# Three small redistributions by way of DRAM instead of TensorE products, in a gated mix of two attention blocks

## The chip, the cores and the metric

The kernel runs on one core of one Trainium2 chip. The metric is the device time of one execution in microseconds (us); lower is better. Before and after are compared by the median of several executions. A profile of one execution gives the times of single instructions. TensorE (PE) does the matrix products and its weight loads (PEld), VectorE (DVE) and ScalarE (ACT) drain its results from PSUM, GpSimd (POOL) works on SBUF, and SyncE (SP) issues nearly all DMA transfers, in one queue.

## The reference

Two full attention blocks run on the same `x` (2048 rows of 640) with their own weights, 32 heads of 20 features each; a sigmoid gate mixes the two results.

```python
def _A_ref(x, wqkv, wo):                      # _B_ref is the same
    qkv = (x @ wqkv).reshape(B, S, 3, H, Dh).transpose(2, 0, 3, 1, 4)
    q, k, v = qkv[0], qkv[1], qkv[2]
    scores = jnp.einsum("bhqd,bhkd->bhqk", q, k) * Dh ** -0.5
    p = _softmax(scores, axis=-1)
    o = jnp.einsum("bhqk,bhkd->bhqd", p, v)
    return o.transpose(0, 2, 1, 3).reshape(B, S, D) @ wo

g = _sigmoid((x * gate_w).sum(-1, keepdims=True))
return g * _A_ref(x, A_wqkv, A_wo) + (1 - g) * _B_ref(x, B_wqkv, B_wo)
```

All arrays are float32; S = 2048, D = 640, H = 32, Dh = 20.

## The kernel before

The two blocks are 16 groups of four heads (8 groups each, `g`). A group goes over four query blocks of 512 (`qb`); one group and query block is a *unit*, 64 in all, numbered here 4g + qb from 0; the second units of the groups are 1, 5, 9 and so on. A unit has eight *steps* (`G`, 512 in all); a step takes 256 keys: scores of four heads for two key tiles, transposed (keys on partitions), in fp16 with each factor split into a high and a low part (L639); the exponential on ACT (L642); and two *values* blocks, the products with V and a column of ones in fp32 that add up in the PSUM bank `acc` (L657). So `acc` ends with each head's weighted values and the sum of its exponentials in row 20 of its 32 rows.

The maximum of each score row has to be known before the exponential, so up to 15 steps ahead (`LEAD`) the kernel computes scores in the other orientation (L576) and reduces them on DVE (L587; half of some by ACT and DVE in pairs, L580 and L584). At the end of a unit's maxima `finish_max` negates them (`mneg`, 128x16), turns them to 16x128, splits them into fp16 parts on POOL, writes these to DRAM (`m_scr`, L613) and reads them (L617) into rows 60 to 63 of each head's part of `QT`, where they are contracted with a constant row of `KT` and so are subtracted inside the score product. Then the unit is *ready*; a step of a unit that isn't ready is not given out, and until then the loop gives out maxima and fill.

The order of the work on all engines is written by a planner when the program is built. Each step follows a written pattern of score halves (e0, e1), maxima (m0, m1), values blocks (V) and slots (X) into which *fill* goes: the projections of the next group's Q, K and V and the output products. Seven PSUM banks are handed out by the planner's clocks. The small chains beside this are generators: each score half calls `advance()`, which takes every generator in `side` one `yield` on (a *turn*, eight per step); a generator that yields `PRODUCT` is parked, and `product()` continues one parked generator ahead of a values block, so that small products stand there. Within one engine's queue the instructions run in the written order, and each waits at the head of its queue for its data.

Three kinds of such chains matter here:
- `take_acc`, once a unit (63 times): ACT copies `acc` to `ot`; a DMA brings the 4x512 sums to 128x16 (`sq`, L748); DVE takes the reciprocal (L750); POOL scales and splits it in two fp16 parts (L752 to L754); two DMAs bring these to 8x512 (`sr`, L758); a product with the selector `sel` spreads them to 32 rows per head (L763); DVE multiplies `ot` by it from PSUM (L765); POOL splits the result for the output product (L768, L769).
- `finish_max`, once a unit (64 times): the turning of `mneg` is a TensorE transpose (L600) and an ACT copy with a scale (L605).
- `scales`, 13 times: the largest magnitude of a set of weights, one column per partition, becomes a power of two on all partitions: transpose (L168), reduction (L172), `powers`, two diagonal matrices (L178), products with ones (L185) and a copy (L188). The first call, for `x` and the first weights, is at the start; the others are for later weights of Q and K (3), of V (7) and of the output (2).

When a group's projections are done, its Q and K are *spread* over partitions for the next group by some 40 DMAs from SP (L423, L425), each with its own turn, near the group's second unit.

Of the kernel before, what the change touches and what calls it, by code (L numbers as in the profile page):

```python
# [10 lines left out]
F16 = mybir.dt.float16  # L11
F32 = mybir.dt.float32
I32 = mybir.dt.int32
# [22 lines left out]
XE = 7  # L36
QKS = 2.0 ** -12
PARTS = (0, 176, 344, 512)
RS = 2.0 ** 13
OB = 3  # L40
OWAIT = 20
SUM0, SUM1 = -8, 1.9
# [9 lines left out]

T_SCORE, T_MODE, T_VALUES, T_READY = 0.217, 0.1, 0.85, 0.39
T_EXP, T_MAX, T_BACK = 0.478, 0.6, 0.15
REST = 6
PRODUCT = "product"
ORDER = (0, 2, 1, 3)
LOW = -3.0e38
MS = 2.0 ** 15
# [3 lines left out]
def kernel(  # L63
# [22 lines left out]
    make_identity(nc, ident)  # L86
    ones = consts.tile([5, P], F32, name="ones")
    nc.vector.memset(ones, 1.0)
    head = consts.tile([2 * GH, GH], F32, name="head")
    nc.gpsimd.tensor_tensor(head, ident[:2 * GH, :GH], ident[:2 * GH, GH:2 * GH], op=OP.add)  # L90
    sel = consts.tile([2 * GH, GH, 32], F16, name="sel")
    nc.vector.tensor_scalar(sel, head.unsqueeze(2).to_broadcast([2 * GH, GH, 32]), 1.0 / RS, None, op0=OP.mult)
    xx = consts.tile([P, 2, NC, S], F16, name="xx")
    xh, xl = xx[:, 0], xx[:, 1]

# [17 lines left out]
    o_scr = [dram.tile([2, D, S], F16, name=f"o_scr{z}") for z in range(2)]  # L113
    m_scr = [dram.tile([4, 16, P], F16, name=f"m_scr{i}") for i in range(2)]
    y_scr = dram.tile([NT, P, D], F32, name="y_scr")


    clock = {"pe": 0.0, "done": 0.0, "act": 0.0, "dve": 0.0}
# [5 lines left out]
    def take():  # L124

        i = min((k for k in range(NB) if k not in held), key=lambda k: free_at[k])
        held.add(i)
        return i, banks[i]
# [33 lines left out]
    def scales(maxima, n, then):  # L162

        for _ in range(REST):
            yield
        yield PRODUCT
        i, pt = take()
        nc.tensor.transpose(pt[:n, :P], maxima[:, :n], ident)  # L168
        tick_block(0.1, free_at[i])
        yield  # L170
        e = wts.tile([5, 8], F32, name="e", tag="scl", bufs=2)
# [4 lines left out]
        dg = wts.tile([5, 2, 5], F32, name="dg", tag="scd", bufs=2)  # L176
        for k in range(2):
            nc.vector.tensor_scalar(dg[:n, k, :n], ident[:n, :n], e[:n, 3 + k:4 + k], None, op0=OP.mult)  # L178
        for _ in range(REST):
            yield  # L180
        yield PRODUCT
        i, pb = take()
        tick_block(0.1, free_at[i])
        for k in range(2):
            nc.tensor.matmul(pb[:, k * n:(k + 1) * n], ones[:n, :], dg[:n, k, :n], start=True, stop=True)  # L185
        yield
# [3 lines left out]
        then(both[:, :n], both[:, n:2 * n])  # L190

    def set_x(r_x, r, inv):
        nc.vector.tensor_copy(r_x, r)
# [80 lines left out]
        return tasks + [last]  # L274

    side = []
    parked = []

    def step_on(gen):

        try:
            return next(gen) is not PRODUCT
        except StopIteration:
            return None

    def advance():
        for gen in list(side):
            goes = step_on(gen)
            if not goes:
                side.remove(gen)  # L290
                if goes is False:
                    parked.append(gen)

    def product():

        if parked:
            gen = parked.pop(0)
            goes = step_on(gen)
            if goes is not None:
                (side if goes else parked).append(gen)  # L300

    def split_weights(t, r, hi, lo, wait=0):

# [287 lines left out]
    def finish_max(g, qb):  # L591

        mneg = wts.tile([P, 16], F32, name="mneg", tag="mneg", bufs=2)
        nc.vector.tensor_reduce(mneg, mparts.pop((g, qb)).rearrange("p a b c d -> p (a b c) d"), axis=AX.X,
                                op=OP.max, negate=True)
        for _ in range(REST):
            yield
        yield PRODUCT
        i, pt = take()
        nc.tensor.transpose(pt[:16, :P], mneg, ident)  # L600
        tick_block(0.1, free_at[i])
        yield
        give(i, spend("act", 0.3, clock["done"]))
        mt = wts.tile([16, P], F32, name="mt", tag="mt", bufs=2)
        nc.scalar.activation(mt, pt[:16, :P], AF.Copy, scale=0.5 / MS)  # L605
        m4 = wts.tile([16, 4, P], F16, name="m4r", tag="m4r", bufs=2)
        for k in range(2):
            nc.gpsimd.tensor_copy(m4[:, k, :], mt)  # L608
        for k in range(2):
            nc.gpsimd.tensor_tensor(m4[:, 2 + k, :], mt, m4[:, 0, :], op=OP.subtract)  # L610
        yield from turns(8)
        ms = m_scr[qb % 2]
        nc.sync.dma_start(ms.rearrange("k r q -> r k q"), m4)  # L613
        yield from turns(5)
        for h in range(GH):
            base, pair = 60 + 64 * (h % 2), h // 2
            nc.sync.dma_start(QT[g % 2][base:base + 4, pair, qb * QB:(qb + 1) * QB],  # L617
                              ms[:, 4 * h:4 * h + 4, :].rearrange("k t q -> k (t q)"))
        ready.add((g, qb))
# [119 lines left out]
    def take_acc(g, qb):  # L739

        ot = work.tile([P, QB], F32, name="ot", bufs=2)
        nc.scalar.activation(ot, acc, AF.Copy)  # L742
        spend("act", T_EXP)
        few, many = (2, 8) if g == 2 * NG - 1 else (6, 24)
        sq = work.tile([P, 16], F32, name="sq", bufs=2)
        sh = work.tile([P, 2, 16], F16, name="sh", bufs=2)
# [3 lines left out]
        nc.vector.reciprocal(sq, sq)  # L750
        spend("dve", 0.25)
        nc.gpsimd.tensor_scalar(sq, sq, RS, None, op0=OP.mult)  # L752
        nc.gpsimd.tensor_copy(sh[:, 0], sq)
        nc.gpsimd.tensor_tensor(sh[:, 1], sq, sh[:, 0], op=OP.subtract)  # L754
        yield from turns(few)
        sr = work.tile([2 * GH, QB], F16, name="sr", bufs=1)
        for k in range(2):
            nc.sync.dma_start(sr[GH * k:GH * k + GH], sh[:, k])  # L758
        yield from turns(many)
        yield PRODUCT  # L760
        i, pt = take()
        tick_block(T_SCORE, free_at[i])
        nc.tensor.matmul(pt, sel.rearrange("k h e -> k (h e)"), sr, start=True, stop=True)  # L763
        yield
        nc.vector.tensor_tensor(ot, ot, pt, op=OP.mult)  # L765
# [3 lines left out]
        nc.gpsimd.tensor_tensor(o[:, 1], ot, o[:, 0], op=OP.subtract)  # L769
# [125 lines left out]
    load, split_next = weights_a(1)  # L895
    load()
    drains = [turn(0, c) for c in range(NC)] + [turn(4, 0)]
    found = []
    run(scales(wm, 5, lambda r, inv: found.extend((r, inv))))
    r, inv = found  # L900
# [63 lines left out]
    def go_on(us):  # L964

        end = clock["pe"] + us
        while clock["pe"] < end and next(rest, PRODUCT) is not PRODUCT:
            pass

    for half in range(2):  # L970
# [150 lines left out]
    for G in range(STEPS + 1):  # L1121
        g, qb, i = unit_of(G)
        now[0] = G
        while G < STEPS and ((g, qb) not in ready or (G and not valued(G - 1))):
            for u, ch in next_maxima(G, 1):
                for j in (1, 0):
                    one_max(u, ch, j)
            finish_step()
            advance()
            product()  # L1130
# [4 lines left out]
        for what in (STEP[blocks] if maxima or some else LATE + " X" * (blocks == 2)).split():  # L1135
# [12 lines left out]
            elif what[0] == "m":  # L1148
                for u, ch in some[(k - 1) * len(some) // 4:k * len(some) // 4]:
                    one_max(u, ch, int(what[1]))  # L1150
            elif what == "V":
                product()
# [8 lines left out]
    while side or parked or fill or current or outs or last:  # L1161
        advance()
        product()
        slot(STEPS)
        out_tasks(STEPS)
    run(last_tiles(NQ - 1, end_o))
# [28 lines left out]
```

## Time and profile before

| | |
|---|---|
| median of 3 executions | 2866.06 us (2865.85 to 2867.37) |
| the profiled execution | 2865.34 us |
| its span, first to last instruction | 2863.5 us |
| granted TensorE clock | 0.997 |
| PE, PEld, DVE, ACT, POOL busy | 2805.2, 982.2, 2405.1, 2567.4, 678.5 us |
| DMA engines' mean busy share | 0.17 |

A row of the groups reads: line, engine, operation, output<-inputs, shapes, count | busy us, mean ns of one | idle time of the engine before them, and what ended it. A row of the timeline reads: start in us, length in us, engine, line, operation, output<-inputs, count of merged instructions. `SPq` is SP's queue: the row is the issue of a transfer, not its landing. Matmuls are pipelined, so that start-to-start times say more of PE than lengths do.

### The profile page before, as it was taken

The page shows a single profiled execution, that of the slowest core. Times are in us where ns is not written, and L with a number is a line of the kernel's source. Part 1 is how long each engine was busy: PE and PEld are TensorE (multiplying, and loading weights), DVE is VectorE, ACT ScalarE, POOL GpSimd, SP SyncE. Part 2 cuts the span into 40 slices and gives each one's busy share as a digit, 9 for nine tenths or more (in the row PEclk, how much of TensorE's full clock was granted, in tenths as well). Part 3 has the DMA queues.
Part 4 walks back from the last instruction along what each step waited for, and adds up shares of the span by engine and source line. Part 5 has one row for each costly group of instructions (what it writes and reads, how often), then busy time and mean ns, then how long its engine had stood idle before and what let it go on. Part 6 is the DMA issues. An engine that isn't in the chain of part 4 may idle for free.

```text
span 2863.5 us, 63124 instructions
## 1 busy us (share of the span) xinstructions
PE 2805.2 (98%) x23489; PEld 982.2 (34%) x23489; DVE 2405.1 (84%) x4637; ACT 2567.4 (90%) x5249; POOL 678.5 (24%) x1103
## 2 busy tenths in 40 slices
PE   6999999999999999999999999999999999999998
PEld 3533223342323323343233333334433333332222
DVE  6688898878898898978988888887788888889982
ACT  3799999989999999989999999998899999888987
POOL 5322113221221212233431111322112233120011
PEclk9999999999999999999999999999999999999999
DMA  4110101001020101202022020210202112221222
GB/s 134 41 38 6 37 10 41 15 15 31 14 52 17 31 15 27 50 10 52 18 45 53 14 60 16 47 37 21 47 21 54 44 35 66 62 72 52 69 61 74
DMA packets 176761, 114.77 MB, mean 40 GB/s; under 512 B 111812, under 2 KB 150396, under 8 KB 176452
## 3 DMA queue, kind: packets, MB, share of 16 engines
q1 hardware_dynamic: 173908, 109.12, 15.9%
q8 instruction: 184, 3.01, 0.4%
q0 software_dynamic: 1600, 0.96, 0.2%
q14 instruction: 125, 1.02, 0.1%
q10 hardware_dynamic: 944, 0.66, 0.1%
HBM read 48.89 MB, written 26.61 MB: 26 GB/s over the span
## 4 chain that ended last, share of the span: by engine, by line
PE 91%; DVE 3%; ACT 2%; DMA 1%; issue 1%; POOL 1%; SPq 0%; POOLq 0%; ACTq 0%; DVEq 0%
PE acc L657 34%; PE bank L639 19%; PE bank L377 19%; PE bank L576 17%; DVE mpart L587 2%; ACT pt L642 1%; PE bank L763 1%; ACT rl L580 1%; PE bank L600 0%; DMA xs<-in_A_x_dram 0%; DMA wv<-in_A_wqkv_dram 0%; DVE rl L584 0%; PE bank L185 0%; ACT ot L742 0%; PE bank L880 0%
## 5 line engine op out<-in xcount | busy, mean ns | idle before, releaser
L642 ACT ACTIVATE pt<-bank 128x512 f32<-128x512 f32 x4096 | 2179.1, 613 | 154.5 <-PE bank L639 85.6
L587 DVE TENSOR_REDUCE mpart<-bank 128x1 f32<-128x512 f32 x2976 | 1883.8, 684 | 337.4 <-PE bank L576 202.8
L657 PE MATMUL acc<-pt,v 128*21 128x512 f32 x8192 | 1081.8, 600 | 2.5 <-ACT ot L742 2.4
L639 PE MATMUL bank<-qt,kt 64*128 64x512 f16 x4096 | 1054.7, 380 | 7.2 <-ACT pt L642 2.9
L576 PE MATMUL bank<-kt,qt 60*128 60x512 f16 x3536 | 1011.0, 380 | 4.6 <-DVE mpart L584 0.9
L576 PEld LDWEIGHTS <-qt 60*128 60x128 f16 x4096 | 235.2, 94 | 679.3 <-issue 621.6
L639 PEld LDWEIGHTS <-kt 64*128 64x128 f16 x4096 | 248.8, 94 | 461.6 <-issue 329.1
L584 DVE CUSTOM_DVE_ANT_0 rl<-bank,rl 128x512 f32<-128x512 f32 x560 | 378.6, 680 | 23.0 <-PE bank L576 9.2
L580 ACT ACTIVATE rl<-bank 128x512 f32<-128x512 f32 x560 | 332.8, 600 | 13.7 <-PE bank L576 11.4
L377 PE MATMUL bank<-xx,wbh 128*128 128x168 f16 (+2 forms) x2240 | 280.0, 244 | 4.5 <-ACT xx L884 1.9
L657 PEld LDWEIGHTS acc<-pt,v 128*21 128x21 f32 x8192 | 143.1, 99 | 403.8 <-issue 384.3
L377 PE MATMUL bank<-xx,wbl 128*128 128x168 f16 (+2 forms) x1120 | 253.0, 243 | 0.0
L768 POOL CAST on<-ot 128x512 f16<-128x512 f32 x63 | 38.5, 611 | 822.6 <-DVE ot L765 796.0
L377 PEld LDWEIGHTS <-wbh 128*128 128x128 f16 x2240 | 184.2, 98 | 87.4 <-issue 80.5
L576 PE MATMUL bank<-kd,qt 60*128 60x512 f16 x560 | 203.5, 381 | 1.6 <-DMA kd<-dd 1.2
L377 PE MATMUL bank<-wvh,xx 128*128 128x160 f16 (+1 forms) x1280 | 155.4, 234 | 0.5 <-ACT rl L580 0.2
L377 PE MATMUL bank<-woh,o_in 128*128 128x160 f16 (+1 forms) x960 | 155.7, 256 | 0.0
L377 PEld LDWEIGHTS <-xx 128*128 128x128 f16 x1920 | 131.9, 97 | 52.2 <-issue 49.0
L377 PE MATMUL bank<-wvl,xx 128*128 128x160 f16 (+1 forms) x640 | 137.3, 231 | 0.6 <-POOL wvl L317 0.6
L608 POOL CAST m4r<-mt 16x128 f16<-16x128 f32 x128 | 33.4, 284 | 437.8 <-ACT mt L605 437.8
L377 PEld LDWEIGHTS <-o_in 128*128 128x128 f16 (+1 forms) x1440 | 104.0, 97 | 75.3 <-issue 62.0
L404 ACT ACTIVATE fs<-bank 128x168 f32<-128x168 f32 (+1 forms) x216 | 69.3, 321 | 52.4 <-PE bank L377 38.7
(137 smaller groups left out, 1395.5 us busy)
## 6 DMA issues: line engine op xcount, KB each, us to landing
y_scr<-y_out SPq DMA_DIRECT2D x32, 320.0 KB
kt<-cq SPq DMA_DIRECT2D x120, 80.0 KB
o_scr<-on SPq DMA_DIRECT2D x240, 40.0 KB
kt<-cq SPq DMA_DIRECT2D x136, 40.0 KB
xs<-in_A_x_dram SPq DMA_DIRECT2D x8, 640.0 KB
o_in<-o_scr SPq DMA_DIRECT2D x32, 160.0 KB
y_out<-y_scr SPq DMA_DIRECT2D x16, 320.0 KB
xx<-y_scr SPq DMA_DIRECT2D x16, 320.0 KB
```

The source lines that it names most:

```text
L377: nc.tensor.matmul(out_ap, a, b, start=(k == 0), stop=(k == len(pairs) - 1))
L404: nc.scalar.activation(f[:, m], pt[:, m], AF.Copy, scale=QKS)
L576: nc.tensor.matmul(pt, QT[g % 2][r, pair, q0:q0 + P], k, start=True, stop=True)
L580: nc.scalar.activation(relus[u, j], pt, AF.Relu)
L584: nc.vector.tensor_tensor_reduce(rl, pt, rl, 1.0, LOW, OP.add, OP.max, m)
L587: nc.vector.tensor_reduce(m, pt, axis=AX.X, op=OP.max)
L608: nc.gpsimd.tensor_copy(m4[:, k, :], mt)
L639: nc.tensor.matmul(et, KT[g % 2][r, pair, kt * P:(kt + 1) * P], QT[g % 2][r, pair, qb * QB:(qb + 1) * QB], start=True, stop=True)
L642: nc.scalar.activation(pt, et, AF.Exp, scale=factor(g // 4))
L657: nc.tensor.matmul(acc[32 * h:32 * h + VW, :], V[(g // 2) % 2][:, kt, (g % 2) * GH + h, :], ptiles.pop((G, kk, h)), start=(kt == 0), stop= ...
L763: nc.tensor.matmul(pt, sel.rearrange("k h e -> k (h e)"), sr, start=True, stop=True)
L768: nc.gpsimd.tensor_copy(o[:, 0], ot)
```

## The change

The three chains above lose their TensorE products in favour of a store to DRAM and a load from it in another layout:
- The reciprocals are stored (`r_scr`, 4x512 in DRAM) and loaded by four broadcast DMAs into 32 rows per head (`rb`); POOL multiplies `ot` by them. The fp16 split, `sr`, `sel` and the product are gone.
- The negated maxima, 128x16, are stored turned (`n_scr`, 16x128), loaded as `mt`, and scaled by POOL. The first unit keeps the transpose and the ACT copy.
- All `scales` but the first store the columns of maxima (`s_scr`), load them back broadcast to all partitions (up to 256 values in each), and DVE reduces them and takes `powers` on every partition. The first is `first_scales`, with the products as before.

`PRODUCT`, `parked` and `product()` are gone. The turns between the parts of the chains change with it: the maxima's chain has 33 to its last load, where it had 20 and a wait for a values block.

```diff
+    s_scr = dram.tile([2, P], F32, name="s_scr")
+    n_scr = [dram.tile([16, P], F32, name=f"n_scr{i}") for i in range(2)]
+    r_scr = [dram.tile([GH, QB], F32, name=f"r_scr{i}") for i in range(2)]
...
     def scales(maxima, n, then):
+        yield from turns(6)
+        nc.sync.dma_start(s_scr[:n].rearrange("k p -> p k"), maxima[:, :n])
+        yield from turns(6)
+        t = work.tile([P, QB], F32, name="fs")[:, :n * P]
+        nc.sync.dma_start(t, s_scr[:n].rearrange("k p -> (k p)").unsqueeze(0).to_broadcast([P, n * P]))
+        yield from turns(12)
+        both = wts.tile([P, 10], F32, name="both", tag="scb", bufs=2)
+        nc.vector.tensor_reduce(both[:, :n], t.rearrange("p (k q) -> p k q", k=n), axis=AX.X, op=OP.max)
+        powers(both.bitcast(I32), n)
+        spend("dve", 1.0)
+        then(both[:, 3 * n:4 * n], both[:, 4 * n:5 * n])
...
     def finish_max(g, qb):
...
-        for _ in range(REST):
+        mt = wts.tile([16, P], F32, name="mt", tag="mt", bufs=2)
+        if now[0] < 0:
             yield
-        yield PRODUCT
-        i, pt = take()
-        nc.tensor.transpose(pt[:16, :P], mneg, ident)
-        tick_block(0.1, free_at[i])
-        yield
-        give(i, spend("act", 0.3, clock["done"]))
-        mt = wts.tile([16, P], F32, name="mt", tag="mt", bufs=2)
-        nc.scalar.activation(mt, pt[:16, :P], AF.Copy, scale=0.5 / MS)
+            i, pt = take()
+            nc.tensor.transpose(pt[:16, :P], mneg, ident)
...
+        else:
+            yield from turns(6)
+            nc.sync.dma_start(n_scr[qb % 2].rearrange("r p -> p r"), mneg)
+            yield from turns(6)
+            nc.sync.dma_start(mt, n_scr[qb % 2])
+            yield from turns(8)
+            nc.gpsimd.tensor_scalar(mt, mt, 0.5 / MS, None, op0=OP.mult)
...
     def take_acc(g, qb):
...
         nc.vector.reciprocal(sq, sq)
         spend("dve", 0.25)
-        nc.gpsimd.tensor_scalar(sq, sq, RS, None, op0=OP.mult)
-        nc.gpsimd.tensor_copy(sh[:, 0], sq)
-        nc.gpsimd.tensor_tensor(sh[:, 1], sq, sh[:, 0], op=OP.subtract)
         yield from turns(few)
-        sr = work.tile([2 * GH, QB], F16, name="sr", bufs=1)
-        for k in range(2):
-            nc.sync.dma_start(sr[GH * k:GH * k + GH], sh[:, k])
+        nc.sync.dma_start(r_scr[qb % 2].rearrange("h (k q) -> (h k) q", q=16), sq)
+        yield from turns(few)
+        rb = work.tile([P, QB], F32, name="rb", bufs=1)
+        for h in range(GH):
+            nc.sync.dma_start(rb[32 * h:32 * h + 32], r_scr[qb % 2][h:h + 1].to_broadcast([32, QB]))
         yield from turns(many)
-        yield PRODUCT
-        i, pt = take()
-        tick_block(T_SCORE, free_at[i])
-        nc.tensor.matmul(pt, sel.rearrange("k h e -> k (h e)"), sr, start=True, stop=True)
-        yield
-        nc.vector.tensor_tensor(ot, ot, pt, op=OP.mult)
-        give(i, spend("dve", 0.7, clock["done"]))
+        nc.gpsimd.tensor_tensor(ot, ot, rb, op=OP.mult)
```

More of the change, by code (lines that the diff above doesn't have):

```diff
@@ L38 @@
 PARTS = (0, 176, 344, 512)
-RS = 2.0 ** 13
 OB = 3
@@ L54 @@
 T_EXP, T_MAX, T_BACK = 0.478, 0.6, 0.15
-REST = 6
-PRODUCT = "product"
 ORDER = (0, 2, 1, 3)
@@ L88 @@
     nc.vector.memset(ones, 1.0)
[L89 to L92, printed above, removed]
     xx = consts.tile([P, 2, NC, S], F16, name="xx")
@@ L160, in powers, with first_scales @@
         nc.vector.tensor_scalar(ei[:, c[4]], ei[:, c[2]], float(XE << 23), None, op0=OP.subtract)
-    def scales(maxima, n, then):
-        for _ in range(REST):
-            yield
-        yield PRODUCT
+    def first_scales(maxima, n):
         i, pt = take()
@@ L169, in scales @@
         tick_block(0.1, free_at[i])
-        yield
-        e = wts.tile([5, 8], F32, name="e", tag="scl", bufs=2)
+        e = wts.tile([5, 8], F32, name="e", tag="scl", bufs=1)
         nc.vector.tensor_reduce(e[:n, 0:1], pt[:n, :P], axis=AX.X, op=OP.max)
@@ L175, in scales @@
         powers(e.bitcast(I32)[:n, :], 1)
-        dg = wts.tile([5, 2, 5], F32, name="dg", tag="scd", bufs=2)
+        dg = wts.tile([5, 2, 5], F32, name="dg", tag="scd", bufs=1)
         for k in range(2):
             nc.vector.tensor_scalar(dg[:n, k, :n], ident[:n, :n], e[:n, 3 + k:4 + k], None, op0=OP.mult)
-        for _ in range(REST):
-            yield
-        yield PRODUCT
         i, pb = take()
@@ L189, in scales @@
         give(i, spend("dve", 0.2, clock["done"]))
-        then(both[:, :n], both[:, n:2 * n])
+        return both[:, :n], both[:, n:2 * n]
+    def scales(maxima, n, then):
+        yield from turns(6)
[9 more added lines that the diff above has]
+        then(both[:, 3 * n:4 * n], both[:, 4 * n:5 * n])
     def set_x(r_x, r, inv):
@@ L276 @@
     side = []
[L277 to L284, printed above, removed]
     def advance():
         for gen in list(side):
-            goes = step_on(gen)
-            if not goes:
+            try:
+                next(gen)
+            except StopIteration:
                 side.remove(gen)
[L291 to L300, printed above, removed]
     def split_weights(t, r, hi, lo, wait=0):
@@ L595, in finish_max @@
                                 op=OP.max, negate=True)
-        for _ in range(REST):
+        mt = wts.tile([16, P], F32, name="mt", tag="mt", bufs=2)
+        if now[0] < 0:
             yield
-        yield PRODUCT
-        i, pt = take()
-        nc.tensor.transpose(pt[:16, :P], mneg, ident)
-        tick_block(0.1, free_at[i])
-        yield
-        give(i, spend("act", 0.3, clock["done"]))
-        mt = wts.tile([16, P], F32, name="mt", tag="mt", bufs=2)
-        nc.scalar.activation(mt, pt[:16, :P], AF.Copy, scale=0.5 / MS)
+            i, pt = take()
+            nc.tensor.transpose(pt[:16, :P], mneg, ident)
+            tick_block(0.1, free_at[i])
+            yield
+            give(i, spend("act", 0.3, clock["done"]))
+            nc.scalar.activation(mt, pt[:16, :P], AF.Copy, scale=0.5 / MS)
+        else:
[5 more added lines that the diff above has]
+            nc.gpsimd.tensor_scalar(mt, mt, 0.5 / MS, None, op0=OP.mult)
         m4 = wts.tile([16, 4, P], F16, name="m4r", tag="m4r", bufs=2)
@@ L745, in take_acc @@
         sq = work.tile([P, 16], F32, name="sq", bufs=2)
-        sh = work.tile([P, 2, 16], F16, name="sh", bufs=2)
         yield from turns(few)
@@ L897 @@
     drains = [turn(0, c) for c in range(NC)] + [turn(4, 0)]
-    found = []
-    run(scales(wm, 5, lambda r, inv: found.extend((r, inv))))
-    r, inv = found
+    r, inv = first_scales(wm, 5)
     r_x = r[:, 4:5]
@@ L966, in go_on @@
         end = clock["pe"] + us
-        while clock["pe"] < end and next(rest, PRODUCT) is not PRODUCT:
+        while clock["pe"] < end and next(rest, 0) is None:
             pass
@@ L1129 @@
             advance()
-            product()
             slot(G)
@@ L1151 @@
             elif what == "V":
-                product()
                 if G:
@@ L1160 @@
     end_o = take_last()
-    while side or parked or fill or current or outs or last:
+    while side or fill or current or outs or last:
         advance()
-        product()
         slot(STEPS)
```

3 lines of the change are left out of this document (removed).

## The prediction

> **What bounds the kernel now.** I read the page's busy times and its chain of work first, then the busy times by stage, then TensorE's timeline around each removed product, then the transfer queue's own timeline.
>
> ```profile
> span 2863.5 us, 63124 instructions
> PE 2805.2 (98%) x23489; PEld 982.2 (34%) x23489; DVE 2405.1 (84%) x4637; ACT 2567.4 (90%) x5249; POOL 678.5 (24%) x1103
> PE 91%; DVE 3%; ACT 2%; DMA 1%; issue 1%; POOL 1%; SPq 0%; POOLq 0%; ACTq 0%; DVEq 0%
> ```
>
> TensorE holds 91% of the chain that ends last; POOL is three quarters idle. Is it so in every stage? Two units of eight steps, by stage (columns: length, then busy PE, PEld, DVE, ACT, POOL, clock, DMA share, GB/s):
>
> ```profile
> 672.00:709.60 37.60, 36.56 (x261) 8.64 (x260) 34.58 (x66) 36.16 (x74) 3.79 (x10) 1.00 0.08 16
> 409.00:451.60 42.60, 42.60 (x381) 15.28 (x381) 36.06 (x67) 39.88 (x82) 12.53 (x19) 1.00 0.08 19
> ```
>
> In the second, usual kind (381 matmuls, with projections between) PE never rests, and DVE and ACT have 6.5 and 2.7 us to spare. In the first (261 matmuls, no projection) PE rests 1.04 us and ACT only 1.44: there PE shares the bound. So time taken from PE is time won nearly everywhere, if nothing new makes PE wait. The clock is 1.00 in both, so no term below hangs on it.
>
> **What the removed products cost on PE.** The timeline of PE (start, length, engine, line, xcount), a values block without a product before it, one behind the sums' product L763, one behind the maxima's transpose L600, one behind a scales product L185:
>
> ```profile
> 1503.30 0.38 PE L576 MATMUL bank<-kt,qt 60*128 60x512 f16 x2
> 1503.61 1.06 PE L657 MATMUL acc<-pt,v 128*21 128x512 f32 x8
> 1508.48 0.38 PE L576 MATMUL bank<-kt,qt 60*128 60x512 f16 x2
> 1508.79 0.38 PE L763 MATMUL bank<-sr,sel 8*128 8x512 f16 x1
> 1509.11 1.05 PE L657 MATMUL acc<-pt,v 128*21 128x512 f32 x8
> 1435.33 0.28 PE L600 MATMUL bank<-ident,mneg 128*16 128x128 f32 x1
> 1435.53 1.06 PE L657 MATMUL acc<-pt,v 128*21 128x512 f32 x8
> 1494.36 0.60 PE L185 MATMUL bank<-dg,ones 1*128 1x1 f32 x4
> 1494.89 1.06 PE L657 MATMUL acc<-pt,v 128*21 128x512 f32 x8
> ```
>
> From the last score to the values block takes 0.31 us without a product (1503.30 to 1503.61) and 0.63 with L763 (1508.48 to 1509.11). A product thus costs its start-to-start time, not its listed length: 0.31 for L763, 0.20 for L600, 0.53 for the four L185 matmuls. How many there are, and what stands beside them on other engines (groups: xcount, busy, mean ns, idle before):
>
> ```profile
> L763 PE MATMUL bank<-sr,sel 8*128 8x512 f16 x63 | 24.0, 381 | 1.2 <-DMA sr<-sh 0.2
> L600 PE MATMUL bank<-ident,mneg 128*16 128x128 f32 x64 | 17.7, 277 | 2.1 <-DVE mpart L587 1.0 <-ACT pt L642 0.3
> L185 PE MATMUL bank<-dg,ones 1*128 1x1 f32 (+2 forms) x52 | 8.2, 259 | 2.9 <-ACT pt L642 1.6 <-DVE dg L178 1.2
> L168 PE MATMUL bank<-ident,m 128*1 128x128 f32 (+1 forms) x12 | 3.2, 270 | 0.5
> L765 DVE TENSOR_TENSOR ot<-ot,bank 128x512 f32<-128x512 f32 x63 | 42.7, 678 | 0.0
> L605 ACT ACTIVATE mt<-bank 16x128 f32<-16x128 f32 x64 | 16.0, 251 | 0.0
> L587 DVE TENSOR_REDUCE mpart<-bank 128x1 f32<-128x512 f32 x2976 | 1883.8, 684 | 337.4 <-PE bank L576 202.8 <-PE bank L639 111.8
> L769 POOL TENSOR_TENSOR on<-ot,on 128x512 f16<-128x512 f32 x63 | 73.1, 1160 | 5.1
> L752 POOL TENSOR_SCALAR sq<-sq 128x16 f32<-128x16 f32 x63 | 16.1, 255 | 416.8 <-DVE sq L750 377.8 <-DVE m L271 13.7 <-DMA qt<-rk 9.4
> ```
>
> 63 x 0.31 = 19.5 us for the sums; 63 x 0.20 = 12.6 for the transposes (the first unit keeps its own); 12 later scales x 0.53 = 6.4 (52 matmuls are 13 times 4, and the first time stays); 12 x 0.20 = 2.4 for L168, taken like L600, whose 128x128 shape it shares. Together **41 us**, the upper term. The idle time that the rows show ahead of these groups (1.2, 2.1 and 2.9) may go as well: 6 us, kept for the low end.
>
> **The other engines.** DVE loses L765 (42.7 us) and in the later scales trades a chain of tiny operations for one reduction of at most 256 columns and four on its columns: nothing. ACT loses 63 L605 (15.8 us). POOL gains a multiplication of 128x512 by 128x512 per unit, priced by L769 at 1.16 us (73 us), and one of 16x128, priced by L752 at 0.25 (16 us), and loses L752 and the two small operations behind it, 16 us at least: it goes from 24% to some 26%, free unless something it delays is awaited. Units like 672.0:709.6 may keep their length, since ACT limits them too. The code projects V for every other group only, so I take a quarter of the first 32 units as bare: 8 x 0.51 = 4 us at most; DVE and ACT shed 0.93 us in each, so I take 2.
>
> **The chain of the maxima.** This is what pays. Before: reduce (L594), transpose, ACT copy, POOL splits, write (L613), four reads (L617), then the unit's first score (L639). After: two more transfers and a POOL multiplication replace transpose and copy. Units 8, 9, 41 and 1, the queue's issue and PE's score:
>
> ```profile
> 420.02 0.22 DVE L594 TENSOR_REDUCE mneg<-mpart 128x16 f32<-128x64 f32 x1
> 427.73 1.26 SPq L617 DMA_DIRECT2D qt<-m_scr  x4
> 451.59 0.39 PE L639 MATMUL bank<-qt,kt 64*128 64x512 f16 x1
> 475.90 1.28 SPq L617 DMA_DIRECT2D qt<-m_scr  x4
> 492.10 0.59 PE L639 MATMUL bank<-qt,kt 64*128 64x512 f16 x2
> 1843.95 1.28 SPq L617 DMA_DIRECT2D qt<-m_scr  x4
> 1855.10 0.39 PE L639 MATMUL bank<-qt,kt 64*128 64x512 f16 x1
> 154.94 1.42 SPq L617 DMA_DIRECT2D qt<-m_scr  x4
> 156.78 0.38 PE L639 MATMUL bank<-qt,kt 64*128 64x512 f16 x1
> ```
>
> Unit 8 stands for the calm units: reads issued 7.7 us after the reduction and 23.9 before the score. Unit 9 (score: second of the pair, 492.32) has 16.4 us, unit 41 has 11.2: both are second units of a group, where the next group's spread (L423, L425) fills SP's queue. Unit 1 has 1.8, and that was enough, so 1.8 us is what a read needs to land.
>
> The price T of the new n_scr write is unknown: 128x16 floats turned to 16x128 is 2048 runs of 4 bytes, and no such store is in the trace. Nearest rows, the 640 four-byte reads of gate_w beside the loads of x (window 3.1 to 5.9), and one 128-run sr transfer (1448.5 to 1448.8), by queue: packets, MB, share; then SP's issue of that sr pair, and of one spread transfer (ns, least, median, most):
>
> ```profile
> q10 hardware_dynamic: 656, 0.00, 13.0%
> q1 hardware_dynamic: 128, 0.00, 23.8%
> 1447.27 1.25 SPq L758 DMA_DIRECT2D sr<-sh  x2
> L423 SPq DMA_DIRECT2D kt<-cq x136: 754/774/1456, 40.1 to 2559.8; - x136
> ```
>
> 656 packets in 2.8 us is 4.3 ns each; 128 in at most 0.3 us is 2.3 ns. Estimate from these: 2048 take 4.7 to 8.7 us, with 1.2 from the issue to the first packet (1447.27 to 1448.5) T = 6 to 10. I take 6, by sr, which SP issues as well and which has no load beside it; both ends stay.
>
> Calm unit: T + 2 (read back) + 2 (multiply, split) + 1.8 (write) = 12 to 16 us from reduction to reads instead of 7.7; 23.9 - 8 still leaves 16. Free. What queues behind SP's wait there (weights, o_in) is asked for many steps ahead.
>
> Second units: the reads now stand some 10 turns later (33 yields, before 20, a PRODUCT and its wait for the next V). In the burst a turn is one spread transfer, 0.8 us with its gap: 8 us; n_scr, mt and four rb issues less one sr add 2; and SP waits for n_scr for s = T less the six transfers between (4.8 us): 1 us. Unit 9: 16.4 - 11 - 1.8 = 3.6 spare. Unit 41: -1.6, a new PE wait. With two or three such units I take **5 us** (0 if T is short and the spread's tail moves up; 40 at T = 10 with half the units as tight as 41).
>
> Unit 1: no slack, ten turns more. Until its maxima are declared ready the loop gives out only maxima and what fill there is; 10 turns at 1.4 us (two L587 of 0.68) = 14 us, of which PE uses about 4 for maxima that are needed later: **10 us** lost (0 if the lead grows in time, 17 if nothing is used).
>
> A sum's reciprocals have 24 turns (some 15 us) between their loads and POOL: hidden. The scales' reduction on DVE stands 12 turns (8 us) behind a broadcast that lands in 2 plus SP's lag: 0, at most 10 in all. The wait would hold DVE's whole queue, hence PE's banks.
>
> **Sum.** -41 + 2 + 10 + 5 = -24. The profiled execution took 2865.34 us (span 2863.5 and 1.84 around it); the median, 2866.06, is 0.7 above. 2866 - 24 = **2842**. 0.2% (5.7 us) is about what this kernel's timing can tell.
>
> A rule that speaks against the change: the Trainium skill, "DMA: Bandwidth & Descriptors", Rules for kernel authors, says that a transfer whose last dimension isn't contiguous becomes one descriptor per element, and its Specifications say that below 512 B the engine reads, modifies and writes. The trace agrees on the first (2.5 KB of gate_w as some 640 packets); no row shows the second for a store. With it T would be the slower rival's.
>
> **Rivals.**
> - *All hidden* (T short, unit 1 finds fill): 2866 - 41 = 2825, with the 6 of idle time 2819. For it: calm slack 23.9. Against: unit 1's 1.8 and unit 41's 11.2.
> - *Another engine takes the bound*: PE's time goes but ACT or DVE holds the step; 2866, no change. For it: 36.16 of 37.60 busy in the unit without projections. Against: 2.7 and 6.5 us free in the usual unit, where most lie.
> - *Slower: the n_scr write blocks SP.* If each four-byte store costs twice gate_w's packet, 2048 x 8.5 ns = 17 us, T = 19, s = 14: unit 9 waits 14 - 4.6 = 9.4 us, some 15 such units 141; calm units still fit (27 of 31.6 us from reduction to score). 2866 - 41 + 12 + 141 = 2978. It decides from s = 6.5, T = 11: then 15 x 1.9 makes up the 29 left. The page's rule on short stores, just named, describes this mechanism.
>
> **How the numbers follow.** Likeliest, 2830 to 2858: 0.53. All hidden, 2817 to 2829: 0.15. No change: 0.11. Slower: 0.21, its worst part past 2890. So faster 0.68, same 0.11, slower 0.21. The range 2817 to 2890 leaves out the deep slow tail (0.15) and a little below; the likeliest case's own range is 2830 to 2858.
>
> **What would show it.** Right: L763, the 63 L600 and the later L168 and L185 gone, 0.31 us from scores to every values block, PE's busy time some 40 us less, waits of PE on qt<-m_scr only in unit 1 and a few second units, POOL near 26%. Wrong: SP waiting for n_scr over 6 us at a time, PE idle before L639 at many unit starts, DVE idle on the scales' broadcast, or ACT holding the chain.

## The result and the profile after

The changed kernel takes **3008.27 us** (median of 4 executions, 3005.59 to 3014.58) against 2866.72 us for the kernel before on the same chip: a ratio of 1.0497, 95% interval 1.0485 to 1.0510, or 142 us slower. Forecast were 2842 us and a range of 2817 to 2890. The profiled execution has a span of 3008.5 us.

The page of the changed kernel (span; busy time of each engine; then groups: busy, mean ns | idle before):

```profile
span 3008.5 us, 62902 instructions
PE 2821.5 (94%) x23303; PEld 976.8 (32%) x23303; DVE 2363.7 (79%) x4537; ACT 2553.3 (85%) x5186; POOL 748.5 (25%) x1039
...
L630 PE MATMUL bank<-qt,kt 64*128 64x512 f16 x4096 | 1070.7, 384 | 41.9 <-DMA qt<-m_scr 19.6
L648 PE MATMUL acc<-pt,v 128*21 128x512 f32 x8192 | 1098.3, 608 | 5.4 <-ACT ot L733 5.3
L561 PE MATMUL bank<-kt,qt 60*128 60x512 f16 x3536 | 1023.5, 384 | 83.3 <-DVE mpart L572 63.3
```

PE runs 186 matmuls fewer (23489 to 23303), as the change says, and yet is busy 16 us longer (2805.2 to 2821.5), so many of its matmuls ran slower: one of the values blocks' (L648) took 608 ns in the mean, before 600, and the granted clock was 0.974, before 0.997. Beside that it is idle for 187 us of the span; before it was 58. Its waits, and those of DVE and of SP's queue, in the changed kernel (total us, times, longest):

```profile
PE bank L561 <- DVE mpart L572: 77.0, 27, 13.0
PE bank L630 <- DMA qt<-m_scr: 19.6, 4, 6.2
...
DVE both L189 <- DMA fs<-s_scr: 63.2, 9, 13.2
...
SPq L594 <- DMA n_scr<-mneg: 309.1, 36, 10.5
...
SPq L186 <- DMA s_scr<-m: 40.6, 10, 7.4
```

SP stands 309 us before the load of `mt` and 41 before the scales' load, for stores to land. PE's waits name DVE's reduction, L572, first, and DVE in turn waits for the scales' broadcast.

**Where it shows, in two places.** First a calm unit, 7. The timeline of the changed kernel around its n_scr store (SP, PE, DVE and ACT; start, length, what ended the idle time):

```profile
442.02 0.39 SPq L592 DMA_DIRECT2D n_scr<-mneg  x1
452.91 0.32 SPq L594 DMA_DIRECT2D mt<-n_scr  x1
...
450.47 0.39 PE L561 MATMUL bank<-kt,qt 60*128 60x512 f16 x1
450.70 0.38 PE L561 MATMUL bank<-kt,qt 60*128 60x512 f16 x1
...
453.45 0.37 PE L561 MATMUL bank<-kd,qt 60*128 60x512 f16 x1 [0.86 <-DVE mpart L572]
...
452.70 1.89 DVE L572 TENSOR_REDUCE mpart<-bank 128x1 f32<-128x512 f32 x3 [2.18 <-PE bank L561]
...
452.74 1.12 ACT L633 ACTIVATE pt<-bank 128x512 f32<-128x512 f32 x2 [1.49 <-PE bank L561]
```

The load's issue waits for the store to land, 10.9 us after the store's issue. What matters is just before that: DVE and ACT are both idle until 452.70 and 452.74, "for PE", whose matmuls had been issued at 450.47 and 450.70 and take 0.4 us. Both engines go on within 0.04 us of each other, and within 0.25 us SP goes on too. PE itself went on issuing until 452.20. No row shows a late computation in between; what comes late is the news of finished work. PE then loses 0.86 us for a bank. It is a loss of a microsecond or so in a unit where the landing itself is well hidden.

Second, the scales in unit 8 (same columns; then two windows: length, busy PE, PEld, DVE, ACT, POOL, clock, DMA share, GB/s):

```profile
505.25 0.43 SPq L183 DMA_DIRECT2D s_scr<-m  x1
513.38 0.35 SPq L186 DMA_DIRECT2D fs<-s_scr  x1
...
517.59 0.29 DVE L189 TENSOR_REDUCE both<-fs 128x1 f32<-128x128 f32 x1 [9.76 <-DMA fs<-s_scr]
...
519.62 0.58 PE L561 MATMUL bank<-kt,qt 60*128 60x512 f16 x1 [9.87 <-DVE mpart L572]
520.13 1.92 PE L648 MATMUL acc<-pt,v 128*21 128x512 f32 x8
```

```profile
509.00:520.00 11.00, 1.07 (x6) 0.12 (x2) 2.26 (x10) 1.79 (x4) 1.27 (x1) 0.63 0.21 42
520.00:526.00 6.00, 6.00 (x29) 1.11 (x30) 4.46 (x10) 3.05 (x6) 5.70 (x6) 0.54 0.31 81
```

The store of 128 neighbouring floats lands after 8.1 us, the broadcast after 4.2 more; DVE stands at the head of its queue for 9.76 us and PE for 9.87. Then PE's clock is 0.54: the eight-matmul values block takes 1.92 us, where it took 1.06. The Trainium skill, "TensorE: Matmul & The Clock Gate", Part 1: The HAM clock gate, says that after an idle window of some 3.4 us the array runs at half rate until such a window has been busy; the trace agrees here, with 0.54 behind 9.87 us of idle PE.

### The profile page after: what moved, and what is told of

Same layout as the page of the kernel before. It is cut to its first block, busy times and chain, and to the rows that moved or that the text cites. A ratio compares the mean times of both kernels' runs of the same rounds, so it can differ in the third digit from the quotient of the medians.

```text
span 3008.5 us, 62902 instructions
## 1 busy us (share of the span) xinstructions
PE 2821.5 (94%) x23303; PEld 976.8 (32%) x23303; DVE 2363.7 (79%) x4537; ACT 2553.3 (85%) x5186; POOL 748.5 (25%) x1039
## 5 line engine op out<-in xcount | busy, mean ns | idle before, releaser
L572 DVE TENSOR_REDUCE mpart<-bank 128x1 f32<-128x512 f32 x2976 | 1880.2, 684 | 446.7 <-PE bank L561 263.4
L630 PE MATMUL bank<-qt,kt 64*128 64x512 f16 x4096 | 1070.7, 384 | 41.9 <-DMA qt<-m_scr 19.6
L648 PE MATMUL acc<-pt,v 128*21 128x512 f32 x8192 | 1098.3, 608 | 5.4 <-ACT ot L733 5.3
L561 PE MATMUL bank<-kt,qt 60*128 60x512 f16 x3536 | 1023.5, 384 | 83.3 <-DVE mpart L572 63.3
L561 PEld LDWEIGHTS <-qt 60*128 60x128 f16 x4096 | 241.7, 95 | 743.2 <-issue 689.2
L596 POOL TENSOR_SCALAR mt<-mt 16x128 f32<-16x128 f32 x63 | 32.8, 521 | 1100.4 <-DMA mt<-n_scr 1100.4
L648 PEld LDWEIGHTS acc<-pt,v 128*21 128x21 f32 x8192 | 143.7, 99 | 468.4 <-issue 455.8
L391 POOL CAST cq<-fs 128x512 f16<-128x512 f32 x60 | 36.5, 608 | 571.8 <-ACT fs L389 569.7
L749 POOL TENSOR_TENSOR ot<-ot,rb 128x512 f32<-128x512 f32 x63 | 80.4, 1276 | 263.5 <-DMA rb<-r_scr 162.9
```

The source lines that it names most:

```text
L391: nc.gpsimd.tensor_copy(hi, f)
L561: nc.tensor.matmul(pt, QT[g % 2][r, pair, q0:q0 + P], k, start=True, stop=True)
L572: nc.vector.tensor_reduce(m, pt, axis=AX.X, op=OP.max)
L596: nc.gpsimd.tensor_scalar(mt, mt, 0.5 / MS, None, op0=OP.mult)
L630: nc.tensor.matmul(et, KT[g % 2][r, pair, kt * P:(kt + 1) * P], QT[g % 2][r, pair, qb * QB:(qb + 1) * QB], start=True, stop=True)
L648: nc.tensor.matmul(acc[32 * h:32 * h + VW, :], V[(g // 2) % 2][:, kt, (g % 2) * GH + h, :], ptiles.pop((G, kk, h)), start=(kt == 0), stop= ...
```

## The experiments

Two theories stood at the start. *Store theory*: the harm is in the stores of neighbouring 4-byte pieces, which land late and disturb others. *Queue theory*: the harm is in the added transfers and waits in SP's and DVE's queues, whatever kind of store they carry. Each kernel is compared with the kernel before on the same chip (2865.9 to 2867.4 us); E1 to E3 are the change's three parts, one at a time.

**E1: the sums alone.** The `take_acc` of the change with `r_scr` and `rb`, in the kernel before:

```diff
-        nc.tensor.matmul(pt, sel.rearrange("k h e -> k (h e)"), sr, start=True, stop=True)
...
+        nc.sync.dma_start(r_scr[qb % 2].rearrange("h (k q) -> (h k) q", q=16), sq)
...
+            nc.sync.dma_start(rb[32 * h:32 * h + 32], r_scr[qb % 2][h:h + 1].to_broadcast([32, QB]))
```

> The kernel before with only the sums' reciprocals spread by way of DRAM (take_acc as in the change). Store theory (the four-byte stores n_scr and s_scr do the harm; none here): 63 x 0.31 us of PE go and nothing replaces them, 2846 to 2851 us. Queue theory (the additional transfers in SP's one queue do the harm; four rb loads of 64 KB a unit stay): the chain of the maxima falls behind them in the second units, 2855 to 2885.

Measured: 2845.68 us, ratio 0.9927 (0.9910 to 0.9943). A gain of 21 us: this part does no harm.

**E2: the maxima alone.** The `finish_max` of the change:

```diff
-        nc.tensor.transpose(pt[:16, :P], mneg, ident)
...
+            nc.sync.dma_start(n_scr[qb % 2].rearrange("r p -> p r"), mneg)
...
+            nc.sync.dma_start(mt, n_scr[qb % 2])
```

> The kernel before with only the negated maxima turned by way of DRAM (finish_max as in the change). Store theory: 2048 four-byte stores a unit land some 11 us after their issue and hold up all engines' semaphores by some 1.3 us a unit, 63 x 1.3 = 80, and unit 1 loses 14: 2866 + 80 + 14 + 10 - 13 = 2940 to 2975. Queue theory: only unit 1 and second units lose, 2866 - 13 + 30: 2870 to 2895.

Measured: 2927.25 us, 1.0211 (1.0191 to 1.0232), between the two forecasts: a loss of 60 us from a part that takes 12.6 us from PE.

**E3: the scales alone.** `first_scales` and `scales` of the change:

```diff
-            nc.tensor.matmul(...)      # L185
...
+        nc.sync.dma_start(s_scr[:n].rearrange("k p -> p k"), maxima[:, :n])
...
+        nc.sync.dma_start(t, s_scr[:n].rearrange("k p -> (k p)").unsqueeze(0).to_broadcast([P, n * P]))
```

> The kernel before with only the later scales by way of DRAM. Store theory: without n_scr ahead of it the s_scr store (128 runs) lands in about 3 us, the broadcast is there before DVE wants it: 2855 to 2870. Queue theory (the broadcast comes late because it stands in the spread's burst in SP's queue): DVE waits 8 to 10 us in six units as in the changed kernel, 2905 to 2930.

Measured: 2890.85 us, 1.0084 (1.0064 to 1.0105), a loss of 24 that missed both forecasts. The 3 us that the store theory gave the s_scr store were wrong: with no n_scr ahead of it, its load still follows 7.5 us later at least and 9.2 in the median of the 12, and DVE waits 25.1 us for the broadcast. The three add up to +63, the whole change is +142.

**E4: the store by itself.** The kernel before, complete with its transposes, and once a unit a store that nothing reads:

```diff
+            nc.sync.dma_start(n_scr[qb % 2].rearrange("r p -> p r"), mneg)
```

> The kernel before, and once a unit SP also stores mneg turned to n_scr in 2048 runs of four bytes; nothing reads it. Store theory: all engines' semaphores pause while the stores land, and PE, DVE and ACT lose some 1 us a unit at the same moment: 2916 to 2960. Queue theory: one more issue of 0.4 us in a queue that has room, nobody waits for it: 2866 to 2876.

Measured: 2931.00 us, 1.0225 (1.0204 to 1.0245). Nothing waits for this store's data, and it costs 64 us, as much as the whole of E2. The queue theory falls for the maxima.

**E5: the same 8 KB, as rows of 64 bytes** (n_scr 128x16, stored as `mneg` lies; against E4).

```diff
-            nc.sync.dma_start(n_scr[qb % 2].rearrange("r p -> p r"), mneg)
+            nc.sync.dma_start(n_scr[qb % 2], mneg)
```

> The kernel before, and once a unit SP stores mneg as it lies, 128 rows of 64 bytes, to DRAM; nothing reads it. If short stores cost by their number (80 ns each on its engine) or by how many meet in one 512-byte line (128 for n_scr, 8 here), this costs little either way: 2866 to 2872. If any additional store in SP's queue costs what e4 showed, 2925 to 2935.

Measured: 2867.74 us, 1.0006 (0.9995 to 1.0016): no cost clear of the noise.

**E6 and E7: the same 2048 four-byte stores, but 512 and 64 bytes apart** (n_scr 16x128x128 and 16x128x16).

```diff
+    n_scr = [dram.tile([16, P, 16], F32, name=f"n_scr{i}") for i in range(2)]    # E7; E6: [16, P, 128]
...
+            nc.sync.dma_start(n_scr[qb % 2][:, :, 0].rearrange("r p -> p r"), mneg)
```

> As e4 (2048 stores of four bytes a unit, nothing reads them), but each goes to a place 512 bytes from the next. Line theory (stores that meet in one line wait for each other, 128 deep): no line is shared, 2866 to 2876. Number theory (each short store costs some 80 ns on its DMA engine wherever it goes): as e4, 2925 to 2935.

> As e6 with places 64 bytes apart. Line theory with lines of 64 bytes or fewer: as e6, 2866 to 2876; with lines of 512 bytes 8 stores still meet in each: 2868 to 2885. Number theory: as e4, 2925 to 2935.

Measured: 2868.14 us, 1.0006 (0.9995 to 1.0016), and 2869.92 us, 1.0009 (0.9999 to 1.0020). So it is neither the number of short stores nor their length. It is that they lie closer together than 64 bytes. E7 also spreads them over 128 KB in place of 8; whether it is the distance of neighbours or the number of pieces in so small a place, these runs don't tell apart. The two kernels E4 and E7 differ in nothing else, and the transfer rows of the 3 us from the store's issue can't tell them apart (packets, MB, share of 16 engines), first E4's, then E7's:

```profile
q1 hardware_dynamic: 2064, 0.01, 30.9%
```

```profile
q1 hardware_dynamic: 2064, 0.01, 30.8%
```

What tells them apart is when the next store lands. SP's timeline in one unit, of E4 and then of E7:

```profile
389.14 0.39 SPq L601 DMA_DIRECT2D n_scr<-mneg  x1
394.77 0.31 SPq L617 DMA_DIRECT2D m_scr<-m4r  x1
400.67 1.26 SPq L621 DMA_DIRECT2D qt<-m_scr  x4
```

```profile
382.16 0.39 SPq L601 DMA_DIRECT2D n_scr<-mneg  x1
387.79 0.31 SPq L617 DMA_DIRECT2D m_scr<-m4r  x1
389.23 1.26 SPq L621 DMA_DIRECT2D qt<-m_scr  x4
```

And SP's waits for m_scr over the whole run (us, times, longest), E4's and then E7's:

```profile
SPq L621 <- DMA m_scr<-m4r: 274.2, 58, 9.2
```

```profile
SPq L621 <- DMA m_scr<-m4r: 66.0, 61, 2.8
```

In both m_scr is stored 5.6 us after n_scr. In E7 it has landed 1.44 us later; in E4 after 5.9, that is 11.5 us after n_scr's issue, though all packets were on record by then. An innocent store, 5 us behind the bad one, lands late with it (a transfer has landed when the wait for it ends). Over the whole run that queue's 303940 packets take 21.4% of the 16 engines' span in E4 and 18.1% in E7: the 4-byte packets take 7.9 and 7.5 ns in the mean, and it is larger packets of other transfers that take longer. In unit 7 of the changed kernel four `o_scr` stores were issued next behind n_scr: there 61 packets keep the engines 67.7% busy from 446 to 450.

How often the news is late can be counted. The trace records each change of a semaphore, a counter by which engines and transfers report finished work. From the first n_scr store to 30 us before the end, the kernel before has no stretch of over 0.9 us without such a change on record, and E7 has none. E4 has 52, 71 us together, all but one of them beginning 7 to 10.4 us behind an n_scr store; the changed kernel has 45.

The Trainium skill, "DMA: Bandwidth & Descriptors", Specifications, sets a bound of 512 B below which the engine reads, modifies and writes. By length alone E5, E6 and E7 would have to suffer too, and they do not: for this cost, the measurement narrows the rule to neighbours closer than 64 B. Its rule of one descriptor per element (Rules for kernel authors) the trace bears out, with 2064 packets for 2048 floats.

**E8: sums and maxima, the turning moved from the store to the load.** The scales keep their products; against E11:

```diff
-    n_scr = [dram.tile([16, P], F32, name=f"n_scr{i}") for i in range(2)]
+    n_scr = [dram.tile([P, 16], F32, name=f"n_scr{i}") for i in range(2)]
-            nc.sync.dma_start(n_scr[qb % 2].rearrange("r p -> p r"), mneg)
+            nc.sync.dma_start(n_scr[qb % 2], mneg)
-            nc.sync.dma_start(mt, n_scr[qb % 2])
+            nc.sync.dma_start(mt, n_scr[qb % 2].rearrange("p r -> r p"))
```

> The kernel before with the sums' part and the maxima's part of the change, but mneg is stored as it lies (128 rows of 64 bytes) and turned by the load (2048 reads of four bytes); the scales keep their products. If short stores and not short transfers are the harm: e1's 2846, less 63 x 0.20 of the transposes, plus some 10 in unit 1: 2832 to 2850. If short reads do the same: 2900 to 2930.

Measured: **2835.30 us**, 0.9889 (0.9872 to 0.9905), faster than both kernels. Its page:

```profile
span 2834.2 us, 63029 instructions
PE 2767.3 (98%) x23363; PEld 971.4 (34%) x23363; DVE 2364.6 (83%) x4573; ACT 2553.7 (90%) x5186; POOL 750.0 (26%) x1039
```

Its timeline, SP in unit 7:

```profile
422.80 0.35 SPq L604 DMA_DIRECT2D n_scr<-mneg  x1
424.80 0.31 SPq L606 DMA_DIRECT2D mt<-n_scr  x1
```

The load is issued 2.0 us after the store, not 10.9, and PE is idle for 67 us of the span in place of 187.

**E9: the changed kernel with the same edit.**

> The changed kernel with one edit: mneg is stored as it lies and turned by the load. If the neighbouring four-byte stores of n_scr are the cause and also what held s_scr and its broadcast up: e8's 2835, less 9 for the scales' products, plus at most the 33 that the scales lost by themselves in e3 (24 + 9): 2835 to 2862. If the scales lose as much by themselves as they do in the changed kernel (some 60 us of DVE's waits and half clock): 2880 to 2900.

Measured: 2862.07 us, 0.9986 (0.9976 to 0.9995). One edit wins back 146 us. Compared with E8, only the scales differ, and they cost 27 us here.

**E10: E9 with the scales' store earlier and the reduction later**, so that DVE should not have to wait (first the turns ahead of the store, then those ahead of the reduction):

```diff
-        yield from turns(6)
+        yield from turns(2)
...
-        yield from turns(12)
+        yield from turns(21)
```

> e9, and the scales' store stands 4 turns earlier, their reduction on DVE 5 turns later (2, 6 and 21 turns instead of 6, 6 and 12). If DVE's wait for the broadcast is what the scales cost: that wait goes, 2824 to 2836. If the s_scr stores (128 neighbours in 8 lines) cost by holding semaphores up: 2836 to 2862, as e9.

Measured: 2877.84 us, 1.0034 (1.0021 to 1.0047), 16 us worse than E9: both forecasts missed. SP's timeline in unit 8 of E9, then its waits over the whole run:

```profile
479.21 0.43 SPq L183 DMA_DIRECT2D s_scr<-m  x1
486.45 0.35 SPq L186 DMA_DIRECT2D fs<-s_scr  x1
495.42 1.48 SPq L608 DMA_DIRECT2D qt<-m_scr  x4
```

```profile
DVE both L189 <- DMA fs<-s_scr: 22.9, 6, 7.3
...
SPq L186 <- DMA s_scr<-m: 34.2, 7, 7.5
```

The same two views of E10, with PE's wait for the maxima:

```profile
477.53 0.43 SPq L183 DMA_DIRECT2D s_scr<-m  x1
485.53 0.35 SPq L186 DMA_DIRECT2D fs<-s_scr  x1
497.72 1.47 SPq L608 DMA_DIRECT2D qt<-m_scr  x4
```

```profile
PE bank L630 <- DMA qt<-m_scr: 23.7, 5, 7.0
...
DVE both L189 <- DMA fs<-s_scr: 7.6, 2, 5.1
...
SPq L186 <- DMA s_scr<-m: 54.5, 10, 7.9
```

DVE's wait fell from 22.9 to 7.6 us as meant, and SP's rose from 34.2 to 54.5: the store takes some 8 us to land, and whatever stands between is used up sooner. Behind SP's wait stand the reads of the next unit's maxima (issued at 495.42 in E9, at 497.72 here), and PE waits 23.7 us for such reads in the whole run, where it waited 4.5 in E9. The wait was moved, not removed.

**E11: the changed kernel with the scales' products back**, so sums and maxima with the turned store.

```diff
-        nc.sync.dma_start(s_scr[:n].rearrange("k p -> p k"), maxima[:, :n])
...
+        nc.tensor.transpose(...); nc.tensor.matmul(...)      # L168, L185
```

> The changed kernel with the scales' products back (sums and maxima by way of DRAM, n_scr stored turned). If the parts add up: 2927 + 2846 - 2867 = 2906, and the scales then cost 102 us in the changed kernel against 24 alone, because their store and broadcast wait behind n_scr. If sums and maxima hinder each other in SP's queue: 2920 to 2990.

Measured: 2951.36 us, 1.0298 (1.0278 to 1.0319). Added up, E1 and E2 would give 2906, so the two parts hinder each other by 45 us; and the scales cost 57 on top of this kernel (3008 less 2951), where alone they cost 24. With the store turned the other way (E8) sums and maxima together gain 31. The hindrance goes with the store. E11 and E8 differ in nothing else, so they show where its 116 us lie. E11's wait of PE for the maxima (us, times, longest):

```profile
PE bank L642 <- DMA qt<-m_scr: 30.8, 7, 5.3
```

In E8 it is 0.9 us, in E2 17.9. E11's seven waits all stand ahead of second units (5, 9, 17, 21, 25, 33 and 53). From one copy of `acc` to the next, units 1 to 63 are 109 us longer than in E8: 54 of it in the 15 first units of groups, at whose ends these waits stand, and 54 in the other 48, 1.1 us each.

**E12: E9 with the scales' maxima in two hops.** Stored 64 bytes apart, turned by a load to one or two partitions, stored as rows of 512 bytes, then broadcast:

```diff
-        nc.sync.dma_start(s_scr[:n].rearrange("k p -> p k"), maxima[:, :n])
-        yield from turns(6)
+        nc.sync.dma_start(s_pad[:, :n], maxima[:, :n])
+        yield from turns(4)
...
+        nc.sync.dma_start(ms, s_pad[:, :n].rearrange("p k -> k p"))
+        yield from turns(4)
+        nc.sync.dma_start(s_scr[:n], ms)
+        yield from turns(4)
```

> The kernel is the changed one with the maxima turned by the load (2862.07 us), and with the scales' maxima stored in rows 64 bytes apart, turned by a load into one or two partitions, stored again as whole rows of 512 bytes, and only then loaded broadcast: three more turns of the queue's time, but no store of neighbouring 4-byte pieces is left anywhere. Against the version that keeps the scales' products (2835.3 us) the loss of 27 us lay in the units that hold a scales store, where SP waited 7.3 to 8 us for it and DVE and PE behind it. Store theory: each hop lands in some 2 us, SP's wait for s_scr and the half-clock stretches in units 8, 16, 24, 32, 40 and 48 go, and with the scales' products gone from PE as well (6.4 and 2.4 us) the time is 2824 to 2838. Broadcast theory: what costs is the broadcast load to 128 partitions and DVE's wait for it at the head of its queue, whatever the store; then the two further transfers make the wait later and the time is 2858 to 2885.

Measured: 2840.59 us, 0.9905 (0.9888 to 0.9921), some 2.6 us above the store theory's range and 17 below the broadcast theory's. Two transfers and two waits more, and 21.5 us less than E9. The same 128 floats, stored 64 bytes apart, are read 1.4 to 4.2 us after the store's issue (2.5 in the median of the 12); in E9 it is 7.1 to 11.8 (8.2). Its page, and then what is left of the broadcast's price in DVE's waits:

```profile
span 2838.4 us, 62949 instructions
PE 2765.6 (97%) x23303; PEld 966.3 (34%) x23303; DVE 2359.6 (83%) x4537; ACT 2552.8 (90%) x5186; POOL 748.5 (26%) x1039
```

```profile
DVE both L195 <- DMA fs<-s_scr: 13.4, 4, 4.3
```

With the products' 8.8 us saved and 5.3 us more time than E8, the scales by way of DRAM still cost some 14 us of other time. DVE's waits of 13.4 are of that size; that they are this cost is not shown.

## Why the prediction was wrong

The miss is 166 us, and two edits account for it: turning `mt` by the load is worth 146, and scales without neighbouring 4-byte stores 21.5. With both, the changed kernel stands at 2840.6, beside the 2842 forecast. So the step that failed is the store's price. That the rest of the sum comes out so near is partly luck: without the scales it gives 2866.5 - 19.5 - 12.6 + 17 = 2851 for E8, which took 2835, 16 us less, and the scales, put at a gain of 8.8 us, cost 5.3 in E12.

- **The price T.** It was taken as 6 us, from packet rates. Over the 63 units the load's issue follows the store's by 9.6 us at least, 11.3 in the median and 14.3 at most. The store's own packets are no guide: E4 and E7 move the same 2064 of them at the same share, and only one has the late landing. A landing time was read from rows that show sending.
- **The price's bearer.** I made T a delay of one chain, with SP's wait as the way in which it reaches others, and called calm units free. E4 shows a cost of 64 us with nobody waiting for that data. Other stores land late with it, and DVE, ACT and SP get the news of finished work late (unit 7, 2.18 and 1.49 us idle). That also goes through units with slack: 1.1 us each in the 48 that aren't first units of a group (E11 less E8).
- **The slower rival.** Its trigger was right (T over 11, SP waiting over 6 us at a time, 309 us in all) and its price wrong: it put 141 us on 15 second units, where PE's waits for `qt<-m_scr` are 13.4 us in three units without unit 1's, and 30.8 in seven in E11, 4.4 us each in place of 9.4. That its 2978 us comes within 30 of the measured time is luck, for the waits of other engines in calm units and the scales, which make up most of the loss, are not in it. The rule on short stores named beside it pointed at the right instruction, but E6 and E7 show that length alone isn't the condition.
- **The scales on DVE.** "0, at most 10 in all" became 63.2 us of DVE waits, the longest 13.2. The mechanism was named (the wait holds DVE's queue, hence PE's banks), the size was not: s_scr's 128 neighbouring floats were not priced as a store at all. With stores 64 bytes apart and in whole rows (E12) it is 13.4, still above the upper bound.
- **The clock.** "No term below hangs on it" failed. From E9 to the changed kernel the span grows by 146.1 us, PE's busy time by 48.9 of them (2772.6 to 2821.5) and its idle time by 97.2. The matmuls are the same 23303 and the granted clock fell from 0.988 to 0.974, so here each us of idle PE came with another half of one in matmuls at a lower clock. E9's page:

```profile
span 2862.4 us, 62902 instructions
PE 2772.6 (97%) x23303; PEld 966.4 (34%) x23303; DVE 2360.3 (82%) x4537; ACT 2552.5 (89%) x5186; POOL 748.6 (26%) x1039
```

- **Right: the products.** All 186 matmuls are gone. The sums' 63 were put at 19.5 us and E1 gained 21. PE's busy time, forecast some 40 us less, is 39.6 less in E12. POOL was put at 26% and is at 26% in E8.
- **The unit limited by ACT.** 2 us were kept for units like 672.00 to 709.60, which "may keep their length". In E8 it takes 36.84 us, where it took 37.60 (36.16 of them ACT busy, now 35.99), so here the term should have been nothing. That unit in E8, by windows:

```profile
671.38:708.22 36.84, 35.57 (x258) 8.37 (x258) 34.00 (x65) 35.99 (x73) 9.58 (x15) 1.00 0.16 31
```

- **Unit 1.** Forecast 10 us. Its first score, at 156.78 before, stands at 172.33 in the changed kernel and 167.84 in E8, where the store lands in 2 us: 11 us later there. Unit 1 itself is then 5.5 us shorter, with 31.6 us of work for DVE in it in place of 40.2: maxima had been done early. Net 5.5 in E8, so half of it was given back. The rows are the changed kernel's, then E8's:

```profile
172.33 0.61 PE L630 MATMUL bank<-qt,kt 64*128 64x512 f16 x1 [6.22 <-DMA qt<-m_scr]
```

```profile
167.84 0.61 PE L642 MATMUL bank<-qt,kt 64*128 64x512 f16 x1
```

- **Second units.** Forecast 5 us at T = 6. At T = 2.0 (E8) PE's waits for `qt<-m_scr` are 0.9 us in all, at T near 11 they are 13.4 beside unit 1's 6.2.

**What stays open.** Why stores that lie closer than 64 B land late, and why engines that do not wait for them learn late of each other's work, no run shows. The distances between 4 and 64 B were not tried, nor other counts than 128 and 2048. How the rest of the 54 us in the first units of groups arises, beyond PE's 30.8 us of waits, is not shown.

## What to carry to other kernels

Turn a small tile by the load, not by the store: store it in whole rows of 64 bytes or more, or put its pieces 64 bytes apart, and gather the 4-byte pieces when reading. Price a store by when its reader may start, not by its packets, and when no row of the trace shows such a store, run it once by itself, unread, before anything is built on it. Where two engines go idle "for PE" and restart together, look for a transfer that lands at that moment; and when a wait is moved to another queue, look at what stands behind it there.

## What was not expected of the hardware

- 2048 four-byte stores to neighbouring addresses land about 11 us after their issue (10.9 in unit 7), and cost 64 us in 63 units with nobody reading them; 64 or 512 bytes apart they cost 3.4 and 1.7 us against the kernel before, and as 64-byte rows 1.3, all within the measurement's uncertainty.
- 128 such stores (s_scr) land in 7.2 us (E9), 8.0 (E10) and 8.1 (the changed kernel) in unit 8, and the read follows all 12 in E9 by 7.1 us or more, so the delay is far from proportional to their number.
- A later, ordinary store lands with them: 5.9 us, not 1.44. Behind the large ones no semaphore changes on record for 0.9 us or more, 52 times in E4 and never in E7.
- Reading the same 2048 floats turned, in 4-byte pieces, has no such price: in E8 all that hangs on it makes PE wait 0.9 us in the whole run.
